# Attention, SwiGLU and maxout layers in one kernel: the first chunk's steps in another order, two more joint score runs, and some weight and softmax work moved between engines

## The chip, the cores and the metric

The kernel runs on one core of one Trainium2 chip. The metric is device time in microseconds. A program on a core drives five engines, each with its own queue of instructions that it works through in order: PE (matrix products), PEld (the same engine's weight loads, which run beside its products), DVE (VectorE), ACT (ScalarE), POOL (GpSimd) and SP (SyncE, which here only issues the transfers). Engines wait for each other and for transfers through semaphores.

## The reference

```python
attn = softmax(where(mask, q @ k.T / 8, -1e9)) @ v     # 4 batches, 8 heads, 576 rows, 64 wide
# heads 0..3: a window of the last 32 rows; heads 4..7: every 32nd row before this one
x = attn.transpose(0, 2, 1, 3).reshape(2304, 512)
g = x @ w_gate; x = (g * sigmoid(g) * (x @ w_val)) @ w_out       # 512 -> 1536 -> 512
out = max(x @ w1, x @ w2, x @ w3) @ w_out2                       # 512 -> 768 -> 512
```

All data is float32. The kernel makes each float32 product from three reduced-precision ones: an operand is split into a high part and a low part, and high times high, high times low and low times high are summed.

## The kernel before, in words

The 2304 rows of `x` are cut into five chunks of 512, 384, 512, 512 and 384 rows. The first chunk is special. No weight is in its final form yet, so while the first chunk is worked on, every weight tile of the SwiGLU layer is loaded as raw words, rounded, and split into its two parts; the later chunks then use them. At the same time the attention of the first two chunks goes through PE.

The order of this whole first stretch is written out by hand as a string, `FIRST`, of about 600 steps; `perform` runs each step once, and the instructions that a step issues are appended to the queues of their engines. So a step's place in the string is its place in every queue that it touches. A step is a letter and a number:

- Attention block i (15 of them; 0 to 3 strided and 4 to 7 local for chunk 0, 8 to 10 local and 11 to 14 strided for chunk 1): `l`/`m` load it (SP), `S` scores on PE (line 475), `M` masked maximum on DVE (line 498), `E` exponentials on ACT (506), `R` inverse of the sums on DVE (511, 512), `N` normalise on DVE or POOL (516), `T` transpose on PE (528), `V` copy out of PSUM on DVE or ACT (533, 535), `P` values product on PE (560), `H` high part of `x` on ACT or DVE (572, 574), `L` low part of `x` on DVE (578).
- Weight tile n (36 of them, in the order in which PE wants them; gate, value and output tiles are called g0, v0, g1, v1, o0, g2, v2, o1, and so on): `r` load the raw words (SP), `a` size (ACT, 291), `q` rounding (ACT, 294), `s` sign (ACT, 300, or POOL, 302), `c` clamp (POOL or DVE, 308), `t` shift (DVE, 314 or 316), `d` rounded sum (DVE, 320), `h` high part (ACT, 335), `o` low part (DVE or POOL, 340), `y` store to DRAM.
- The layer itself for tile f: `G`/`b` gate product on PE (748 to 750, into `ps_g`), `u` tanh on ACT (805), `w` silu on DVE (809), `B` value product on PE (`ps_v`), `x` their product on DVE (813), `z`/`j` high and low part (ACT 782, DVE 786), `O` output product on PE (`ps_y`).

A product of one tile is 12 matmuls of 512 columns: four steps of lines 748, 749 and 750, which need, in this order, the high parts of both operands, the low part of `x` (or of `h`), and the low part of the weight tile. `G0` is cut in two: `G0` does its first half, `b0` the second half after attention blocks 4 to 7 are done, and right behind it come `B0`, `G1`, `B1` and `O0`. Two PSUM buffers hold gate and value products, so `G1` can start when `w0` has read the product of `G0`.

`W` i scores blocks i and i + 1 in one run, with their products interleaved (`scores_beside`); the kernel before does so for blocks 13 and 14 alone.

Which engine does a step is set by seven tuples: `ON_SCALAR` (signs), `EVICT_ON_VECTOR` (`V`), `HIGH_ON_VECTOR` (`H`), `NORM_ON_POOL` (`N`), `CLAMP_ON_VECTOR` (`c`) and `LOW_ON_POOL` (`o`) among them. The string `LATER`, for the other chunks, and the last layer are the same in both kernels.

Of the kernel before, what the change touches and what calls it, by code (L numbers as in the profile page):

```python
# [51 lines left out]


FIRST = """
l0 k0 l1 l2 l3 l4 m4 k1 l5 m5 r0 l6 m6 l7 m7 r1 r2 r3 r4 S0 M0 S1 E0 M1 S2 R0 E1 N0 M2 S3 E2 R1 T0 M3 N1 S4 V0
E3 R2 T1 P0 N2 M4 V1 T2 R3 P1 E4 V2 N3 H0 S5 L0 T3 H1 M5 P2 V3 E5 L1 P3 R4 N4 H3 a0 S6 R5 q0 c0 L3 T4 H2 M6 N5
s0 t0 T5 L2 E6 S7 d0 V5 h0 M7 P5 V4 R6 E7 P4 o0 N6 G0 a1 R7 H5 N7 T6 H4 L5 a2 l8 L4 c1 T7 V6 q1 s1 r5 V7 q2 P6
c2 a3 P7 t1 H6 r6 q3 s2 L6 S8 H7 d1 s3 L7 c3 m8 h1 b0 t2 r7 a4 o1 q4 d2 a5 B0 t3 c4 r8 h2 M8 c5 u0 o2 s4 r9 w0
E8 d3 G1 x0 r10 h3 t4 t5 z0 o3 q5 y1 d4 a6 j0 s5 B1 R8 s6 l9 h4 d5 u1 r13 o4 q7 h5 N8 q6 w1 c6 O0 r12 a7 o5 s7
t6 x1 c7 m9 a8 d6 q8 r11 T8 t7 c8 z1 G2 V8 d7 h6 y3 j1 h7 o6 a9 o7 q9 r14 P8 s8 a10 c9 S9 u2 t8 l10 H8 B2 s9 M9  # L60
c10 y4 L8 a11 d8 E9 w2 c11 r15 t10 O1 x2 h8 q11 R9 m10 o8 z2 N9 r17 q10 t9 s11 T9 j2 G3 s10 d9 r16 t11 V9 d10 h9
d11 y7 a12 o9 h10 P9 h11 s12 B3 y6 u3 o10 H9 o11 q12 L9 c12 S10 a13 w3 y9 q13 c13 a14 t12 M10 s13 x3 c14 O2 r21
q14 s14 z3 t13 E10 d12 r18 d13 G4 j3 h12 R10 h13 r19 o12 a15 N10 q15 t14 y10 a16 T10 o13 u4 B4 d14 V10 w4 c15
r20 s15 c16 t15 q16 s16 h14 y12 d15 P10 a17 o14 q17 O3 x4 c17 H10 l11 h15 t16 r23 s17 L10 z4 d16 y13 o15 G5 h16
j4 q18 m11 l12 m12 o16 a18 r24 s18 t17 c18 a19 d17 S11 u5 y15 t18 c19 B5 w5 h17 M11 q19 r22 o17 a20 d18 E11 t19
s20 y16 x5 G6 c20 h18 R11 t20 z5 N11 s19 r26 j5 q20 T11 o18 a21 O4 d20 r25 V11 d19 q21 h20 c21 h19 o20 r27 s21
t21 P11 S12 o19 a22 B6 d21 H11 l13 l14 u6 c22 L11 y19 h21 s22 w6 q22 o21 q23 r28 t22 O5 a24 x6 s23 c24 m13 m14
d22 z6 y18 q24 s24 h22 j6 a23 o22 G7 r29 a25 M12 c23 q25 t24 E12 r31 t23 c25 d24 W13 s25 d23 y21 B7 h24 R12 M13
h23 N12 u7 y22 o23 E13 w7 t25 T12 M14 r32 a26 o24 O6 V12 R13 s26 x7 q26 c26 r30 a27 N13 z7 t26 q27 d25 P12 r33
a28 j7 G8 h25 d26 H12 o25 s27 L12 c27 y24 h26 c28 t27 a29 T13 o26 q29 r34 B8 d27 V13 s28 u8 s29 c29 w8 y25 t28  # L70
h27 q28 t29 o27 a30 O7 r35 x8 s30 q30 d28 z8 y27 c30 h28 j8 a31 o28 q31 G9 d29 q32 y28 s31 c31 t30 h29 t31 E14
d30 O8 d31 u9 o29 h30 R14 h31 o30 a32 N14 y30 a33 w9 B9 s32 q33 o31 a34 c32 y31 q34 c33 s33 t32 T14 a35 x9 c34
G10 V14 t33 s34 z9 d32 q35 j9 h32 d33 s35 P13 P14 o32 u10 B10 t34 h33 w10 c35 H13 H14 d34 L13 L14 h34 o33 O9 o34
y33 x10 t35 z10 y34 j10
"""
# [1255 lines left out]
```

## Time and profile before

| what | value |
|---|---|
| median of three runs | 779.96 us (779.40 to 781.55) |
| the profiled execution's own time | 779.35 us |
| its span, first to last instruction | 777.6 us, so 1.75 us lie around it |
| PE busy in the span | 763.9 us (98%) |
| DVE, ACT, POOL busy | 614.0, 457.3, 169.3 us |

The span is cut by what PE does: up to 23.74 us there is attention alone and PE often waits; from 23.74 to 34.92 us lies the first gate and value product; from 34.92 to 139.57 us the rest of the first chunk; behind it the other chunks and the last layer. A row of a timeline gives start, length, engine, line, operation, output and inputs, their shape, and in brackets the idle time ahead of it with what ended it. A matmul's length overlaps the next one's: what a matmul costs PE is the distance from its start to the next start.

### The profile page before, as it was taken

What the parts mean: (1) busy time and instruction counts of PE and PEld (TensorE: products, weight loads), DVE (VectorE), ACT (ScalarE), POOL (GpSimd) and SP (SyncE); (2) the same over time, 40 slices, a digit from 0 to 9 for tenths busy, and PEclk for the clock granted to TensorE, in tenths of its full rate; (3) what the DMA queues carried; (4) which work ended last, traced back from release to release, by engine and by line L of the source; (5) the groups of instructions that cost most, each with busy time, mean ns of one, the idle gap of its engine ahead of it and who ended that gap; (6) DMA issues with size and microseconds to landing.
All of it is one profiled execution on the core that took longest, in us unless ns stands there. A gap on an engine that the chain in (4) does not pass through costs nothing.

```text
span 777.6 us, 13127 instructions
## 1 busy us (share of the span) xinstructions
PE 763.9 (98%) x4644; PEld 695.2 (89%) x4644; DVE 614.0 (79%) x1218; ACT 457.3 (59%) x990; POOL 169.3 (22%) x165
## 2 busy tenths in 40 slices
PE   6999999999999999999999999999999999999998
PEld 4677788999988888888888999999999999999998
DVE  5999999888899989999999963626688377856683
ACT  6999997666857757477787752423345233443332
POOL 2434332111221121111121211411124011321120
PEclk9999999999999999999999999999999999999999
DMA  9979875576645976636978699996775976879722
GB/s 284 364 257 330 306 298 208 153 263 233 227 138 169 347 228 213 205 130 223 360 240 314 205 366 332 400 376 249 279 260 203 418 272 250 284 286 352 274 96 82
DMA packets 72290, 203.60 MB, mean 262 GB/s; under 512 B 8640, under 2 KB 40320, under 8 KB 67616
## 3 DMA queue, kind: packets, MB, share of 16 engines
q1 hardware_dynamic: 72224, 202.76, 73.7%
q8 instruction: 37, 0.61, 0.3%
q14 instruction: 29, 0.24, 0.1%
HBM read 158.69 MB, written 44.04 MB: 261 GB/s over the span
## 4 chain that ended last, share of the span: by engine, by line
PE 91%; DMA 3%; DVE 2%; ACT 2%; POOL 1%; issue 0%; SPq 0%; ACTq 0%; DVEq 0%
PE ps_a L913 19%; PE ps_c L913 10%; PE ps_v L748 6%; PE ps_y L748 6%; PE ps_g L748 6%; PE ps_y L749 6%; PE ps_y L750 6%; PE ps_g L750 6%; PE ps_v L750 6%; PE ps_g L749 6%; PE ps_v L749 6%; PE ps_b L913 5%; PE ps_a L560 1%; PE ps_a L528 1%; PE ps_a L475 1%; DMA qke<-in_locqk_dram 1%
## 5 line engine op out<-in xcount | busy, mean ns | idle before, releaser
L924 ACT ACTIVATE s<-ps_a 128x384 f32<-128x384 f32 x99 | 48.5, 490 | 132.9 <-PE ps_a L913 132.9
L786 POOL TENSOR_TENSOR hl<-ht,hh 128x512 fp32r<-128x512 f32 (+1 forms) x47 | 62.8, 1336 | 289.7 <-ACT hh L782 283.6
L748 PE MATMUL ps_g<-xh,wh_g 128*128 128x512 f32 (+1 forms) x240 | 90.2, 376 | 1.1 <-DVE ht L809 1.1
L748 PE MATMUL ps_v<-xh,w_v 128*128 128x512 f32 (+1 forms) x240 | 90.3, 376 | 0.5 <-DMA w_v<-wvdr 0.5
L748 PE MATMUL ps_y<-hh,w_o 128*128 128x512 f32 (+1 forms) x240 | 89.6, 373 | 0.0
L749 PE MATMUL ps_g<-xl,wh_g 128*128 128x512 f32 (+1 forms) x240 | 88.4, 368 | 0.2 <-DVE xl L578 0.2
L750 PE MATMUL ps_v<-xh,w_v 128*128 128x512 f32 (+1 forms) x240 | 88.4, 369 | 0.0
L750 PE MATMUL ps_y<-hh,w_o 128*128 128x512 f32 (+1 forms) x240 | 88.4, 368 | 0.0
L749 PE MATMUL ps_y<-hl,w_o 128*128 128x512 f32 (+1 forms) x240 | 88.4, 368 | 0.0
L750 PE MATMUL ps_g<-xh,wl_g 128*128 128x512 f32 (+1 forms) x240 | 88.4, 368 | 0.0
L749 PE MATMUL ps_v<-xl,w_v 128*128 128x512 f32 (+1 forms) x240 | 88.3, 368 | 0.0
L782 ACT ACTIVATE hh<-ht 128x512 fp32r<-128x512 f32 (+1 forms) x60 | 35.1, 585 | 41.2 <-DVE ht L777 30.2
L777 DVE SCALAR_TENSOR_TENSOR ht<-ht,ps_v 128x384 f32<-128x384 f32 (+1 forms) x48 | 29.6, 618 | 31.8 <-PE ps_v L750 28.5
L913 PE MATMUL ps_a<-y0hT,wr 128*128 128x384 f32 x162 | 54.1, 334 | 0.0
L913 PE MATMUL ps_a<-y1hT,wr 128*128 128x384 f32 x162 | 54.1, 334 | 0.0
L748 PEld LDWEIGHTS ps_g<-xh,wh_g 128*128 128x128 f32 x240 | 45.1, 188 | 7.5 <-DVE ht L809 1.5
L769 ACT ACTIVATE ht<-ps_g 128x384 f32<-128x384 f32 (+1 forms) x48 | 26.1, 545 | 43.1 <-PE ps_g L750 42.6
L748 PEld LDWEIGHTS ps_v<-xh,w_v 128*128 128x128 f32 x240 | 45.1, 188 | 6.9 <-issue 0.8
L750 PEld LDWEIGHTS ps_v<-xh,w_v 128*128 128x128 f32 x240 | 45.0, 188 | 6.2 <-DVE w_v L340 0.5
L750 PEld LDWEIGHTS ps_y<-hh,w_o 128*128 128x128 f32 x240 | 45.0, 188 | 6.0 <-DVE w_o L340 0.3
L749 PEld LDWEIGHTS ps_g<-xl,wh_g 128*128 128x128 f32 x240 | 45.1, 188 | 5.8 <-DVE xl L578 0.5
L750 PEld LDWEIGHTS ps_g<-xh,wl_g 128*128 128x128 f32 x240 | 45.1, 188 | 5.8
(255 smaller groups left out, 2062.4 us busy)
## 6 DMA issues: line engine op xcount, KB each, us to landing
wr<-wsdr SPq DMA_DIRECT2D x36, 1792.0 KB, 7.6
raw<-in_w_dram SPq DMA_DIRECT2D x60, 512.0 KB, 6.5
w_v<-wvdr SPq DMA_DIRECT2D x36, 512.0 KB, 5.7
w_o<-wodr SPq DMA_DIRECT2D x36, 512.0 KB, 4.4
wsdr<-whi SPq DMA_DIRECT2D x36, 256.0 KB, 4.2
wvdr<-w_v SPq DMA_DIRECT2D x12, 512.0 KB, 4.8
wodr<-w_o SPq DMA_DIRECT2D x12, 512.0 KB, 4.5
wsdr<-w SPq DMA_DIRECT2D x24, 256.0 KB, 3.7
```

Source lines behind the costliest of these rows:

```text
L475: yield nc.tensor.matmul(self.s[self.half[j], g], self.q[r, u, a], self.k[r, u, a], start=True, stop=True)
L528: nc.tensor.transpose(ps[:sm.shape[2], g * 128:(g + 1) * 128], sm[:, g], ident)
L560: ins = nc.tensor.matmul(ps[j * D:(j + 1) * D, at:at + nq], v, p, start=True, stop=True).ins
L748: nc.tensor.matmul(ps, wh, xh, start=first, stop=False)
L749: nc.tensor.matmul(ps, wh, xl, start=False, stop=False)
L750: nc.tensor.matmul(ps, wl, xh, start=False, stop=last)
L769: nc.scalar.activation(t, gates.pop((c, f)), AF.Silu)
L777: nc.vector.scalar_tensor_tensor(t, t, 1.0, vals.pop((c, f)), ALU.mult, ALU.mult)
L782: nc.scalar.activation(hs[c, f][0], t, AF.Copy)
L786: eng.tensor_tensor(hl, held.pop(("t", c, f)), f32(hh), ALU.subtract)
L913: nc.tensor.matmul(ps, w[:, c, a, ks], b, start=first and n == q == 0, stop=last and n == len(wts) - 1 and q == 2, skip_group_check=True,)
L924: nc.scalar.activation(s, ps, AF.Copy)
```

## The change

The string `FIRST` is replaced by another one with the same work in a new order, in which `W8` stands for `S8` and `S9`, and `W11` for `S11` and `S12`. The tuples change as follows.

```diff
-E3 R2 T1 P0 N2 M4 V1 T2 R3 P1 E4 V2 N3 H0 S5 L0 T3 H1 M5 P2 V3 E5 L1 P3 R4 N4 H3 a0 S6 R5 q0 c0 L3 T4 H2 M6 N5
-s0 t0 T5 L2 E6 S7 d0 V5 h0 M7 P5 V4 R6 E7 P4 o0 N6 G0 a1 R7 H5 N7 T6 H4 L5 a2 l8 L4 c1 T7 V6 q1 s1 r5 V7 q2 P6
-c2 a3 P7 t1 H6 r6 q3 s2 L6 S8 H7 d1 s3 L7 c3 m8 h1 b0 t2 r7 a4 o1 q4 d2 a5 B0 t3 c4 r8 h2 M8 c5 u0 o2 s4 r9 w0
+T1 P0 N2 T2 V1 M4 R3 E4 S5 P1 H0 V2 N3 a0 T3 M5 V3 P3 P2 L0 S6 R4 H1 c0 S7 L1 H3 E5 R5 m6 q0 N4 H2 s0 N5 m7 M6
+L3 t0 E6 T5 d0 T4 V5 M7 V4 R6 P5 L2 h0 P4 a1 N6 E7 R7 H5 L5 o0 G0 a2 T6 r6 H4 a3 V6 q4 N7 c1 T7 L4 q2 P6 q1 l8
+H6 s1 c2 V7 P7 q3 t1 L6 H7 c3 l9 d1 s3 s2 W8 t2 a4 r5 L7 d2 h1 m9 b0 o1 a6 t3 M8 B0 r9 a5 h2 u0 r11 w0 s4 o2 G1
...
-ON_SCALAR = (0, 3, 4, 5, 7, 9, 10, 11, 13, 15, 17, 18, 19, 21, 23, 25, 27, 29, 31, 33, 35)
+ON_SCALAR = (0, 3, 4, 5, 7, 9, 10, 11, 13, 15, 17, 18, 19, 21, 23, 25, 27, 29, 31, 32, 33, 34, 35)
...
-EVICT_ON_VECTOR = (0, 2, 3, 5, 6, 7)
-HIGH_ON_VECTOR = (0, 3)
-NORM_ON_POOL = (0, 1, 2, 3, 4, 5, 6, 7)
+EVICT_ON_VECTOR = (3, 5, 6, 7, 9, 14)
+HIGH_ON_VECTOR = (0, 3, 4, 11, 13)
+NORM_ON_POOL = (1, 3, 4, 5, 7, 8, 10, 12, 13)
...
-CLAMP_ON_VECTOR = ()
-LOW_ON_POOL = ()
+CLAMP_ON_VECTOR = (11, 23, 25, 27, 30, 34)
+LOW_ON_POOL = (0, 1, 3, 4, 6, 8, 16, 17, 19, 21, 29, 30, 32)
```

By these tuples the low parts of 13 weight tiles go from DVE to POOL, the clamps of 6 from POOL to DVE, and two signs from POOL to ACT; three normalisations go from POOL to DVE and four the other way.

First place: PE around `b0`, the second half of the first gate product. Before, the run of scores ahead of it is `S8` alone:

```order
L528 MATMUL ps_a<-cst,qke 96x128 x8
L560 MATMUL ps_a<-qke,ve 64x64 x16
L475 MATMUL ps_a<-loct 64x96 x8
L748 MATMUL ps_g<-xh,wh_g_433 128x512
L749 MATMUL ps_g<-xl,wh_g_433 128x512
```

Now it is `W8`:

```order
L528 MATMUL ps_a<-cst,qke 96x128 x8
L560 MATMUL ps_a<-qke,ve 64x64 x16
L475 MATMUL ps_a<-loct 64x96 x16
L748 MATMUL ps_g<-xh,wh_g_449 128x512
L749 MATMUL ps_g<-xl,wh_g_449 128x512
```

The 8 score products of block 9 have moved up into the run ahead of `b0`; their own run, after the second gate product of the dense stretch, is gone. In the same way the runs of blocks 11 and 12 become one run of 16 where block 11's was, and the run of block 10 now stands right behind `P9`, where it was one product later by itself.

Second place: POOL from the normalisation of block 7 (`qke`, 128x384, the last of its kind) on. `w32_...` is a weight tile in work: before, 475, 489, 518, 563 and 569 are v0, g1, v1, o0 and g2.

```order
L516 TENSOR_TENSOR qke_181<-qke_181,state_183 128x384
L308 TENSOR_SCALAR w32_475<-w32_475 128x512
L302 TENSOR_SCALAR raw_186<-raw_186 128x512
L308 TENSOR_SCALAR w32_489<-w32_489 128x512
L302 TENSOR_SCALAR raw_188<-raw_188 128x512
L308 TENSOR_SCALAR w32_518<-w32_518 128x512
L308 TENSOR_SCALAR w32_563<-w32_563 128x512
L308 TENSOR_SCALAR w32_569<-w32_569 128x512
```

Now 462, 482, 493, 497 and 603 are the same five tiles, and the row before the normalisation is the low part of g0:

```order
L340 TENSOR_TENSOR wl_g0_450<-w32_335,wh_g0_449 128x512
L516 TENSOR_TENSOR qke_192<-qke_192,state_194 128x384
L308 TENSOR_SCALAR w32_462<-w32_462 128x512
L302 TENSOR_SCALAR raw_204<-raw_204 128x512
L308 TENSOR_SCALAR w32_482<-w32_482 128x512
L308 TENSOR_SCALAR w32_493<-w32_493 128x512
L302 TENSOR_SCALAR raw_206<-raw_206 128x512
L340 TENSOR_TENSOR w_v0_567<-w32_462,w_v0_567 128x512
L308 TENSOR_SCALAR w32_497<-w32_497 128x512
L308 TENSOR_SCALAR w32_603<-w32_603 128x512
L308 TENSOR_SCALAR w32_578<-w32_578 128x512
L340 TENSOR_TENSOR w_v1_644<-w32_493,w_v1_644 128x512
```

The sign of g1 (`raw_206`, step `s2`) now has one more clamp ahead of it, that of v1, and the low parts of g0, v0 and v1 stand in this queue.

Third place: DVE at the same time. `xl` is the low part of `x`; before, the two `xl` rows are `L6` and `L7`, and `ps_a_520` is block 7's:

```order
L316 SCALAR_TENSOR_TENSOR w32_475<-w32_475,raw_186 128x512
L578 TENSOR_TENSOR xl_297<-ps_a_507,xh_296 128x2x128
L320 ISA w32_475<-w32_475,q_474 128x1024
L578 TENSOR_TENSOR xl_297<-ps_a_520,xh_296 128x2x128
L316 SCALAR_TENSOR_TENSOR w32_489<-w32_489,raw_188 128x512
L340 TENSOR_TENSOR w_v0_551<-w32_475,w_v0_551 128x512
L320 ISA w32_489<-w32_489,q_488 128x1024
L314 TENSOR_SCALAR w32_518<-w32_518 128x512
...
L340 TENSOR_TENSOR wl_g1_589<-w32_489,wh_g1_588 128x512
L809 SCALAR_TENSOR_TENSOR ht_598<-ht_598,ps_g_467 128x512
```

Now `ps_a_524` is block 7's:

```order
L316 SCALAR_TENSOR_TENSOR w32_462<-w32_462,raw_204 128x512
L578 TENSOR_TENSOR xl_295<-ps_a_508,xh_294 128x2x128
L320 ISA w32_462<-w32_462,q_461 128x1024
L316 SCALAR_TENSOR_TENSOR w32_482<-w32_482,raw_206 128x512
L578 TENSOR_TENSOR xl_295<-ps_a_524,xh_294 128x2x128
L320 ISA w32_482<-w32_482,q_481 128x1024
L314 TENSOR_SCALAR w32_493<-w32_493 128x512
...
L809 SCALAR_TENSOR_TENSOR ht_608<-ht_608,ps_g_474 128x512
L340 TENSOR_TENSOR wl_g1_606<-w32_482,wh_g1_605 128x512
```

`L7` has gone behind the shift of g1 (line 316 on `w32_482`), the low part of v0 has left this queue, and the silu of tile 0 (line 809) now stands ahead of the low part of g1.

## Rows read from the trace of the kernel before

**Rows 1.** The page's first part: busy time (share of the span) of each engine.

```profile
PE 763.9 (98%) x4644; PEld 695.2 (89%) x4644; DVE 614.0 (79%) x1218; ACT 457.3 (59%) x990; POOL 169.3 (22%) x165
```

**Rows 2.** Busy time by stage: PE, PEld, DVE, ACT, POOL, clock, DMA share, GB/s.

```profile
0.00:23.74 23.74, 15.94 (x240) 12.59 (x241) 14.44 (x97) 16.89 (x74) 5.52 (x15) 0.93 0.95 308
23.74:34.92 11.18, 9.68 (x84) 6.91 (x80) 10.25 (x26) 10.45 (x25) 8.00 (x9) 1.00 0.98 341
34.92:70.00 35.08, 34.77 (x206) 27.61 (x207) 34.02 (x73) 33.49 (x74) 13.19 (x16) 1.00 0.85 292
70.00:139.57 69.57, 69.49 (x460) 55.51 (x459) 67.20 (x140) 58.14 (x127) 22.58 (x28) 1.00 0.78 280
139.57:777.60 638.03, 633.97 (x3664) 592.61 (x3660) 488.13 (x885) 338.34 (x693) 120.03 (x99) 1.00 0.72 255
```

**Rows 3.** What PE waited for: us in total, times, longest.

```profile
PE ps_a L528 <- POOL qke L516: 1.6, 2, 1.0
PE ps_g L748 <- DVE ht L809: 1.1, 1, 1.1
PE ps_a L528 <- DVE sm L516: 0.3, 1, 0.3
```

**Rows 4.** PE's timeline: score runs of one block and of two.

```profile
47.27 0.88 PE L475 MATMUL ps_a<-loct 64*64 64x96 f32 x16
48.08 0.50 PE L748 MATMUL ps_v<-xh,w_v 128*128 128x512 f32 x1
48.41 0.39 PE L749 MATMUL ps_v<-xl,w_v 128*128 128x512 f32 x1
48.65 0.39 PE L750 MATMUL ps_v<-xh,w_v 128*128 128x512 f32 x1
...
76.98 0.67 PE L475 MATMUL ps_a<-loct 64*64 64x48 f32 x16
...
96.12 0.68 PE L475 MATMUL ps_a<-loct 64*64 64x48 f32 x32
...
138.75 0.89 PE L475 MATMUL ps_a<-loct 64*64 64x96 f32 x32
```

**Rows 5.** PE's timeline: second step of `b0`, and the start of `G1`.

```profile
29.33 0.50 PE L749 MATMUL ps_g<-xl,wh_g 128*128 128x512 f32 x1 [0.19 <-DVE xl L578]
34.92 0.50 PE L748 MATMUL ps_g<-xh,wh_g 128*128 128x512 f32 x1 [1.11 <-DVE ht L809]
```

**Rows 6.** DVE's timeline between `L7` and `w0`.

```profile
28.86 0.41 DVE L578 TENSOR_TENSOR xl<-ps_a,xh 128x256 fp32r<-128x256 f32 x1
29.49 0.69 DVE L316 SCALAR_TENSOR_TENSOR w<-w,raw 128x512 int32<-128x512 int32 x1 [0.21 <-POOL raw L302]
30.10 1.10 DVE L340 TENSOR_TENSOR w_v<-w,w_v 128x512 fp32r<-128x512 f32 x1
...
33.59 0.68 DVE L340 TENSOR_TENSOR wl_g<-w,wh_g 128x512 fp32r<-128x512 f32 x1
34.20 0.67 DVE L809 SCALAR_TENSOR_TENSOR ht<-ht,ps_g 128x512 f32<-128x512 f32 x1
```

**Rows 7.** POOL's timeline: the sign of g1, then three clamps in a row.

```profile
28.48 0.98 POOL L302 TENSOR_SCALAR raw<-raw 128x512 f32<-128x512 f32 x1
29.53 3.15 POOL L308 TENSOR_SCALAR w<-w 128x512 f32<-128x512 f32 x3
```

**Rows 8.** Two-operand work on POOL in later chunks: by form (busy, mean ns), and two single rows.

```profile
L786 POOL TENSOR_TENSOR hl<-ht,hh 128x512 fp32r<-128x512 f32 x24 | 36.2, 1506 | 164.0 <-ACT hh L782 164.0
...
238.85 1.29 POOL L786 TENSOR_TENSOR hl<-ht,hh 128x512 fp32r<-128x512 f32 x1 [5.99 <-ACT hh L782]
...
273.09 2.42 POOL L786 TENSOR_TENSOR hl<-ht,hh 128x512 fp32r<-128x512 f32 x1 [7.70 <-ACT hh L782]
```

**Rows 9.** DVE's timeline beside those two: one 128x1088 product each.

```profile
239.15 2.14 DVE L657 TENSOR_TENSOR pr<-stk,stq 128x1088 f32<-128x1088 f32 x1
...
273.06 1.28 DVE L688 TENSOR_TENSOR pr<-stv,stsc 128x1088 f32<-128x1088 f32 x1
```

More of the change, by code (lines that the diff above doesn't have):

```diff
@@ L54 @@
 FIRST = """
-l0 k0 l1 l2 l3 l4 m4 k1 l5 m5 r0 l6 m6 l7 m7 r1 r2 r3 r4 S0 M0 S1 E0 M1 S2 R0 E1 N0 M2 S3 E2 R1 T0 M3 N1 S4 V0
-E3 R2 T1 P0 N2 M4 V1 T2 R3 P1 E4 V2 N3 H0 S5 L0 T3 H1 M5 P2 V3 E5 L1 P3 R4 N4 H3 a0 S6 R5 q0 c0 L3 T4 H2 M6 N5
-s0 t0 T5 L2 E6 S7 d0 V5 h0 M7 P5 V4 R6 E7 P4 o0 N6 G0 a1 R7 H5 N7 T6 H4 L5 a2 l8 L4 c1 T7 V6 q1 s1 r5 V7 q2 P6
-c2 a3 P7 t1 H6 r6 q3 s2 L6 S8 H7 d1 s3 L7 c3 m8 h1 b0 t2 r7 a4 o1 q4 d2 a5 B0 t3 c4 r8 h2 M8 c5 u0 o2 s4 r9 w0
-E8 d3 G1 x0 r10 h3 t4 t5 z0 o3 q5 y1 d4 a6 j0 s5 B1 R8 s6 l9 h4 d5 u1 r13 o4 q7 h5 N8 q6 w1 c6 O0 r12 a7 o5 s7
@@ L60 @@
[L60 to L74, printed above, removed]
+l0 k0 l1 l2 l3 S0 l4 S1 k1 l5 r0 l7 l6 M0 r1 r2 E0 m5 M1 S2 E1 m4 R0 r3 S3 M2 r4 N0 E2 R1 T0 M3 R2 V0 S4 N1 E3
@@ new lines @@
+T1 P0 N2 T2 V1 M4 R3 E4 S5 P1 H0 V2 N3 a0 T3 M5 V3 P3 P2 L0 S6 R4 H1 c0 S7 L1 H3 E5 R5 m6 q0 N4 H2 s0 N5 m7 M6
+L3 t0 E6 T5 d0 T4 V5 M7 V4 R6 P5 L2 h0 P4 a1 N6 E7 R7 H5 L5 o0 G0 a2 T6 r6 H4 a3 V6 q4 N7 c1 T7 L4 q2 P6 q1 l8
+H6 s1 c2 V7 P7 q3 t1 L6 H7 c3 l9 d1 s3 s2 W8 t2 a4 r5 L7 d2 h1 m9 b0 o1 a6 t3 M8 B0 r9 a5 h2 u0 r11 w0 s4 o2 G1
+c4 d3 t4 E8 x0 r15 c5 c6 r7 r8 h3 d4 q5 o3 z0 s5 u1 h4 m8 s6 q8 t5 a7 r13 o4 B1 r10 c7 R8 d5 N8 j0 h5 q7 q6 O0
+t6 w1 o5 T8 x1 a8 d6 r12 s7 z1 c8 h6 q9 t7 d7 a10 M9 y3 V8 s8 j1 G2 h7 t8 a9 r14 o6 y4 a11 o7 P8 B2 u2 s9 l10 w2
@@ new lines @@
+d8 H8 c10 r17 c9 c11 L8 O1 x2 E9 y1 h8 o8 t10 q11 R9 z2 N9 q10 T9 y6 G3 t9 s10 s11 d9 t11 h9 V9 a12 P9 d11 d10
+m10 o9 q17 s12 h11 j2 S10 y7 h10 u3 H9 o11 L9 c12 q12 B3 o10 a13 O2 r20 q13 w3 c13 a14 y9 t12 M10 c14 x3 G4 s13
+r16 E10 r19 t13 q14 z3 d12 r18 r21 s14 d13 h12 R10 q15 j3 o12 N10 h13 T10 t14 a16 o13 a15 c15 u4 B4 w4 l11 q16
+c16 y10 y13 d14 s15 V10 h14 y12 t15 d15 a17 o14 P10 O3 x4 a21 s16 t16 s17 H10 r23 l12 h15 c17 G5 z4 d16 h16 q18
+m11 o16 a18 a19 s18 c18 t17 u5 L10 j4 o15 d17 l13 W11 y15 c19 r28 t18 r24 B5 h17 m12 M11 o17 t19 w5 q19 r22 a20
@@ new lines @@
+d18 G6 E11 s20 x5 q20 c20 R11 z5 t20 r26 N11 h18 r30 d20 T11 j5 s19 O4 r25 q21 d19 h20 r27 h19 y16 V11 c21 s21
+t21 o20 o19 o18 a22 d21 P11 s22 H11 L11 u6 h21 w6 l14 B6 q22 q23 c22 t22 a24 s23 x6 q24 o21 z6 a23 y19 y18 O5
+d22 c24 j6 h22 s24 t24 m13 r29 m14 o22 a25 G7 M12 c23 c25 q25 E12 t23 d24 s25 u7 W13 r31 d23 t25 R12 h23 M13 B7
+N12 y21 o23 y22 E13 w7 T12 M14 r32 h24 a26 V12 O6 q26 R13 a31 P12 o24 x7 c26 a27 s26 N13 z7 d25 h25 q27 a28 t26
+d26 r33 c27 G8 s27 q29 H12 h26 c28 o25 a29 t27 u8 d27 L12 T13 V13 o26 s28 c29 j7 B8 y24 s29 w8 q30 t29 t28 q28
@@ L75 @@
+h27 a30 O7 x8 s30 d28 d29 z8 c31 r35 h28 a32 c30 q31 j8 o28 G9 t30 r34 o27 E14 O8 s31 h29 u9 q33 y28 d30 t31 y27
+h30 R14 a33 d31 h31 N14 w9 q32 B9 x9 o29 o31 s32 q34 c32 s33 c33 a34 T14 o30 t32 q35 G10 z9 a35 V14 t33 d32 c34
+j9 s34 P14 P13 H13 d33 h32 c35 s35 t34 H14 u10 B10 d34 w10 t35 o32 L14 y30 O9 h34 h33 o33 x10 o34 z10 y25 L13
+y34 j10 y31 y33
 """
```

## The prediction, on record before the result

> **What bounds the kernel now.** I read the busy times first: PE is busy for 763.9 us [rows 1]. The table by stage says where the rest is [rows 2]. Behind 139.57 us PE idles for 4.1 of 638 us; the steps there are the same in both kernels, so what the first chunk gains or loses there is simply added to the end. From 34.92 to 139.57 us PE idles for 0.31 + 0.08 us. The idle time that this change can reach lies before: 7.8 us up to 23.74, and 1.5 us (11.18 - 9.68) between 23.74 and 34.92. Most of the 7.8 us is the wait for the first transfers and then a chain of small softmax steps.
>
> So there are two questions. Does PE get less to do in the first chunk? And do the engines that make the weights still deliver in time? The second is tight: from 34.92 to 70 us DVE is busy for 34.02 of 35.08 us and ACT for 33.49 [rows 2]. They are as full as PE, and only PE's own order hides it. From 70 us on ACT falls to 84% (58.14 of 69.57) and POOL has room throughout.
>
> The waits name two narrow places [rows 3]: `G1` waited 1.1 us for the silu of tile 0, and a transpose 0.3 us for the normalisation of block 9 on DVE. The DVE rows show why the silu was late [rows 6]: the shift of g1 waited until the sign of g1 on POOL ended (28.48 + 0.98 = 29.46 [rows 7]); then the low part of v0 took 1.02 us from start to next start instead of 0.6, because three clamps ran on POOL beside it; the low part of g1 and the silu followed, and the silu ended at 34.8. `G1` started at 34.92 [rows 5].
>
> **The change part by part.** *Joint runs.* A run of one local block lasts 0.88 us and one of two 0.89; one of a strided block 0.67 and one of two 0.68 [rows 4]. A run overlaps the next matmul by 0.07 (47.27 + 0.88 against 48.08). `W8` and `W11` each save one run: 0.81 + 0.60 = **-1.4 us** of PE time. The bounds are these rows; nothing else in PE's work changes, since the other runs only stand elsewhere.
>
> *Interruptions.* Behind a score run the first matmul costs 0.33 us to the next start, the second 0.24 [rows 4]: an interruption costs 0.1 us. Block 10's scores now stand behind another small run, so the stretch has one interruption less, as the new order on PE shows: **-0.1 us**. Blocks 9 and 12 stood beside other small runs already.
>
> *Block 9.* Its scores come some 18 us earlier (47.27 [rows 4] against the 29.33 of [rows 5], ahead of which `W8` stands), its maximum and exponentials some steps earlier on DVE and ACT. The 0.3 us that its transpose waited go: **-0.3 us**, bounds -0.3 and 0. `W8` takes both PSUM buffers of this kind; the one of block 9 is given back by its maximum, ahead of `V8` on DVE, and only `P8` is queued for it, so I put that at nothing. If the maximum is late, `P8` and all PE work behind it wait.
>
> *The start, 23.74 to 34.92.* This is the term that I can bound and not fix. In the new order `L7` stands behind the shift of g1 on DVE, and that shift needs the sign of g1 on POOL. Let X be the time at which that sign ends. Then come the shift (0.6, start to start), `L7` (0.34, from the 0.41 of its row less the overlap), the five remaining steps of `b0` (5 x 0.23) and `B0` (12 x 0.23): G1 starts at X + 4.9. DVE no longer holds it up, since the low part of v0 (1.02) has left its queue and the silu stands 0.6 us further ahead. Before, X was 29.46 and `G1` came at 34.92, so the new order breaks even at X = 30.0.
>
> What is X now? Ahead of that sign POOL has one clamp more (between 0.6 and 1.05; the three clamps in 3.15 us are the upper end [rows 7]) and the low part of g0 (1.29 to 2.42, mean 1.51 [rows 8]), but no longer the normalisation of block 6, and the scores of blocks 6 and 7 stand together on PE, ahead of the transposes of 4 and 5. I followed the new rows of all engines with these durations twice, once with the scores at the start slow and every POOL row beside DVE at its upper end, once without: X = 30.1 and X = 28.8. I take the middle, 29.5: **-0.5 us**. The bounds: 1.5 us better if all idle time of this stage goes, and 2 us worse if X is 32 (below).
>
> *Lows on POOL, clamps on DVE.* Thirteen lows leave DVE, 0.6 us each. But beside a two-operand POOL instruction a 128x1088 product on DVE took 2.14 us; beside another it took 1.28, and then the POOL instruction took 2.42 instead of 1.29 [rows 8, 9]. Whichever loses, one of them loses about a microsecond. At 0.86 us lost on DVE for each 0.6 us taken off it, 13 lows make DVE's work 3.4 us longer; at none lost, 7.8 us shorter. The lows of DVE stand between instructions that read PSUM, so I take half the loss: DVE gains 13 x (0.6 - 0.43) = 2.2 us in 100. The six clamps cost it 0.34 us each, a shift's length (2.0 us), and spare it the same collisions. So DVE comes out level. This is where a rule of the Trainium skill speaks against the change: GPSIMD Engine Reference, "Key points", says that GpSimd shares its SBUF interfaces with VectorE and contends with its instructions that have two SBUF inputs. The trace agrees, with the 2.14 against 1.28 us; by the rule alone DVE would take the whole loss, which is the slower rival below.
>
> *The rest of ACT, DVE, POOL.* ACT gets two evictions and two signs, and gives up two evictions and three high parts; POOL gives up three normalisations and gets four. Level again, so ACT stays at 95% until 70 us, and can run ahead by no more than its idle 1.6 us. PE, 2 us earlier, will meet a tile that is not ready: I charge **+0.4 us**, bounds 0 and 1.3 (all that is gained before 70 us: 0.81 + 0.1 + 0.3, rounded up).
>
> *Transfers.* The raw words of v0 and g1 go ahead of the values of blocks 4 to 7. By the shapes, 5.07 MB are queued up to the values of block 4, at 308 GB/s [rows 2] some 16.5 us, and they are needed at about 21; those of 6 and 7 are 6.51 MB, 21.1 us, needed at 26. The raw words of o1 and g3 go behind those of three later tiles, 1.5 MB or 5 us, and are not wanted before 41 us. Nothing, if that holds.
>
> Sum: -1.4 - 0.1 - 0.3 - 0.5 + 0.4 = **-1.9 us**. The profiled execution took 779.35 us (777.6 and 1.75 around it), so 777.45; the median of the runs is 0.6 above it: **778.0 us**, 0.25% less. A measurement of this kernel tells no less than about 0.3% (2.3 us) from no change.
>
> **The rivals.** *The start gains too* (chance 0.36). X is 28.5 or less, all idle time between 23.74 and 34.92 goes (-1.5), and the weights keep up: -1.4 - 0.1 - 0.3 - 1.5 = -3.3, 776.7 us. For it: DVE has 1.6 us less ahead of the silu. Against: three full engines before 70 us.
>
> *The weights set the pace* (0.16). PE waits for ACT and DVE until 70 us and only `W11` and the lost interruption remain: -0.7, 779.3 us. For it: the 97% and 95% [rows 2]. Against: PE hardly waited before, at the same load.
>
> *GpSimd holds the start* (0.11, slower). Every POOL row beside DVE takes its upper end, the low of g0 2.42 us and each clamp and sign 1.05. From 25.3 us for the first clamp, 1.1 later for that low, five rows of 1.13: X = 32.05, `G1` at 36.95, +2.0. Then three more clamps, the lows of v0, v1 and o0 at 2.5 and a sign follow X: 12 us, 44.1, where `O0` wants the last at 42.9: +1.2 more. With -1.8 from the first three terms: +1.4, 781.4 us, and 782.4 where two further lows (v2, g3) lose 0.5 us each. It decides from X = 31.8 on, where the start has lost all of the -1.8. For it: the two rows of rows 8. Against: the low of g0 leaves POOL before the softmax of block 7 is there.
>
> **How the numbers follow.** My forecast has 0.37, and its own range is 777.0 to 779.0. Faster by over 0.3% is the first rival and the edge of the forecast: 0.38. Slower is the last one, which reaches 782.3 only in part; with what I have not seen, 0.11. Within 0.3%: 0.51. The range leaves out 0.1 at either end: 776.2 to 780.8.
>
> **What would show it.** In the changed profile: score runs of 0.89 and 0.68 us at `W8` and `W11`; no wait of the transpose for block 9; the end of the sign of g1, and `G1` 4.9 us behind it; `L749` of `b0` waiting for `L7`; lows on POOL of 1.3 to 2.4 us. I am wrong if PE waits for a low part on POOL (line 340) for more than half a microsecond in all, if PE idles for over 1 us between 35 and 70 us, or if anything behind 139 us changes its length.

## The result: slower, and the profile after

The changed kernel takes 784.91 us (median of six runs, 783.75 to 787.11) where the kernel before takes 779.83: a ratio of 1.0056, 95% interval 1.0035 to 1.0078. The forecast was 778.0, and its range ended at 780.8. The profiled execution is the longest of the six: 787.11 us, span 785.3.

The page's first part gives busy time (share of the span) of each engine; PE does its 763 us of work as in [rows 1], and the span is 7.7 us longer.

```profile
PE 763.2 (97%) x4644; PEld 694.3 (88%) x4644; DVE 618.3 (79%) x1213; ACT 458.0 (58%) x989; POOL 186.5 (24%) x171
```

Cut at the same times as [rows 2], with the same columns:

```profile
0.00:23.74 23.74, 15.16 (x245) 12.11 (x246) 15.38 (x101) 18.80 (x81) 5.36 (x14) 1.00 0.95 320
23.74:34.92 11.18, 9.01 (x96) 6.94 (x95) 9.37 (x24) 9.48 (x24) 8.88 (x10) 1.00 1.04 364
34.92:70.00 35.08, 32.77 (x186) 26.07 (x185) 34.77 (x68) 32.61 (x69) 23.23 (x20) 1.00 0.77 268
70.00:139.57 69.57, 67.39 (x420) 52.85 (x420) 67.58 (x137) 58.56 (x125) 29.84 (x30) 1.00 0.71 264
139.57:785.30 645.73, 638.83 (x3703) 596.38 (x3701) 491.19 (x888) 338.51 (x693) 119.19 (x99) 1.00 0.72 254
```

From 34.92 to 139.57 us PE idles for 2.31 + 2.18 us where it idled for 0.39. DVE has given 13 low parts away and is busier than before: 34.77 of 35.08 us against 34.02. That row is the prediction's failure in one line. What PE waits for from `G1` on (us, times, longest), where [rows 3] had 0.3 us:

```profile
PE ps_a L528 <- DVE sm L516: 1.8, 2, 1.1
PE ps_y L749 <- DVE hl L786: 0.9, 2, 0.8
PE ps_g L748 <- ACT sm L506: 0.9, 1, 0.9
PE ps_a L560 <- ACT w_o L335: 0.9, 1, 0.9
```

By place, with the waits as PE's timeline brackets them: `O0` 0.76, `P8` 0.85, `T9` 0.69, `G6` 0.87, `T14` 1.11, `O10` 0.17. Two of these are put down to ACT, at `P8` and `G6`; both went when nothing but DVE steps was put forward ("Three places of the order" below). No wait names a low part on POOL (line 340): the harm goes through DVE. In POOL's timeline (start, length) the sign of g1 ends at 29.15, and four low parts follow, those beside `b0`, `O0`, `T9` and `T14`:

```profile
28.49 0.66 POOL L302 TENSOR_SCALAR raw<-raw 128x512 f32<-128x512 f32 x1
29.36 1.65 POOL L340 TENSOR_TENSOR w_v<-w,w_v 128x512 fp32r<-128x512 f32 x1 [0.22 <-ACT w_v L335]
...
38.38 1.85 POOL L340 TENSOR_TENSOR w_o<-w,w_o 128x512 fp32r<-128x512 f32 x1 [0.45 <-ACT w_o L335]
...
41.34 1.15 POOL L516 TENSOR_TENSOR sm<-sm,stat 128x384 f32<-128x384 f32 x1
...
52.20 1.57 POOL L340 TENSOR_TENSOR wl_g<-w,wh_g 128x512 fp32r<-128x512 f32 x1 [2.93 <-ACT wh_g L335]
...
57.04 3.10 POOL L302 TENSOR_SCALAR raw<-raw 128x512 f32<-128x512 f32 x1 [3.26 <-ACT w L291]
...
120.99 1.60 POOL L340 TENSOR_TENSOR w_v<-w,w_v 128x512 fp32r<-128x512 f32 x1
```

And DVE's timeline at the same moments:

```profile
38.99 1.79 DVE L786 TENSOR_TENSOR hl<-ht,hh 128x512 fp32r<-128x512 f32 x1
...
41.72 0.68 DVE L809 SCALAR_TENSOR_TENSOR ht<-ht,ps_g 128x512 f32<-128x512 f32 x1
...
52.54 1.26 DVE L511 TENSOR_SCALAR stat<-stat 128x4 f32<-128x4 f32 x1
...
57.73 0.68 DVE L340 TENSOR_TENSOR w_v<-w,w_v 128x512 fp32r<-128x512 f32 x1
58.33 0.68 DVE L786 TENSOR_TENSOR hl<-ht,hh 128x512 fp32r<-128x512 f32 x1
58.93 0.68 DVE L340 TENSOR_TENSOR wl_g<-w,wh_g 128x512 fp32r<-128x512 f32 x1
...
121.37 1.43 DVE L516 TENSOR_TENSOR sm<-sm,stat 128x192 f32<-128x192 f32 x1
```

Read them in pairs by their ends. The low part of 38.38 ends at 40.23; the `hl` of 38.99, which alone takes 0.68, ends at 40.78, and `O0` goes on at 40.84. The one of 52.20 ends at 53.77; a sum over four columns, 0.16 us alone, ends at 53.80, and `T9` is late by what follows. The one of 120.99 ends at 122.59; the normalisation of block 14 at 122.80. A DVE instruction that starts while POOL works ends a fixed time after POOL's, 0.55 us for two 512-column inputs, 0.28 for one, 0.02 for four columns: it waits until POOL has ended, and then does its own work. All 38 DVE rows between 24 and 142.60 us that are over 0.05 us longer than the shortest of their form end in this way. The silu at 41.72, one of whose inputs lies in PSUM, takes its 0.68 us beside POOL's 41.34. And at 57.04 it is POOL that waits, 3.10 us for a sign, while DVE works without a gap.

### The profile page after: what moved, and what is told of

It is laid out like the page before. It is cut to its first block, busy times and chain, and to the rows that moved or that the text cites. A ratio compares the mean times of both kernels' runs of the same rounds, so it can differ in the third digit from the quotient of the medians.

```text
span 785.3 us, 13096 instructions
## 1 busy us (share of the span) xinstructions
PE 763.2 (97%) x4644; PEld 694.3 (88%) x4644; DVE 618.3 (79%) x1213; ACT 458.0 (58%) x989; POOL 186.5 (24%) x171
## 4 chain that ended last, share of the span: by engine, by line
PE 80%; DVE 2%; DMA 1%; ACT 1%; issue 0%; SPq 0%; ACTq 0%; DVEq 0%
PE ps_a L913 19%; PE ps_c L913 10%; PE ps_y L749 5%; PE ps_y L748 5%; PE ps_v L748 5%; PE ps_y L750 5%; PE ps_v L750 5%; PE ps_v L749 5%; PE ps_g L748 5%; PE ps_b L913 5%; PE ps_g L750 5%; PE ps_g L749 5%; DMA wsdr<-s 1%; PE ps_a L560 1%; PE ps_a L528 1%; PE ps_a L700 1%
## 5 line engine op out<-in xcount | busy, mean ns | idle before, releaser
L320 DVE CUSTOM_DVE_ANT_0 w<-w,q 128x1024 uint16<-128x1024 uint16 x60 | 50.9, 854 | 4.2 <-ACT q L300 2.5
L748 PEld LDWEIGHTS ps_v<-xh,w_v 128*128 128x128 f32 x240 | 45.2, 188 | 9.6 <-DVE y0lT L268 2.9
L749 PEld LDWEIGHTS ps_y<-hl,w_o 128*128 128x128 f32 x240 | 45.4, 189 | 7.5 <-DVE hl L786 2.2
```

Source lines behind the costliest of these rows:

```text
L320: nc.vector.tensor_tensor(w, w, q, ALU.add)
L748: nc.tensor.matmul(ps, wh, xh, start=first, stop=False)
L749: nc.tensor.matmul(ps, wh, xl, start=False, stop=False)
```

## Experiments

Behind each text: the median, the ratio to the kernel before on the same chip (95% interval), and **the stretch**, the time from the start of `G1` to the start of chunk 1. The stretch is the sharpest measure here: two executions of the kernel before's first chunk gave 104.65 and 104.62 us, two of the changed one's 108.36 and 108.44. The start of `G1` scatters far more (33.17 to 34.92 for the same first chunk), and so do the runs. The stretch has a limit too: it leaves out what is lost ahead of `G1`, and where `G1` came at 37 us or later, in three of the runs below, the makers of the weights had 2 to 4 us more for their work.

**Lows back on VectorE.**

```diff
-LOW_ON_POOL = (0, 1, 3, 4, 6, 8, 16, 17, 19, 21, 29, 30, 32)
+LOW_ON_POOL = ()
```

> The changed kernel with its 13 low parts of weight tiles back on VectorE. Theory A (the low parts on GpSimd slow the two-operand instructions of VectorE beside them, and PE waits for what is queued behind): the 4.1 us of new waits between 35 and 140 us go, chunk 1 starts near 138.5 us instead of 142.6, and the time is 777 to 780 us. Theory B (the new order puts single steps too late, whatever engine makes the low parts): the waits ahead of P8, T9, G6 and T14 stay, 783 to 786 us. Theory C (VectorE has too much to do in either case, 7.8 us more of it here): slower than the change, 786 to 790 us.

785.65 us, 1.0072 (1.0050 to 1.0094), stretch 108.13. Not A: the order wants them away from DVE. The waits ahead of `P8`, `T9` and `T14` are gone; `O0` waits 1.17 us, `G6` 0.52 and other places 1.44, which is 3.13 in all, and all but the 0.52 is named after DVE. So most of B's waits aren't there, although the time lies in its range, and C's range begins above it: none of the three fits, and C's reason, too much work on DVE, comes nearest. Ahead of the stretch PE waited 2.06 us at 25.83 for the low part of g0, now on DVE; the granted clock was then 0.55 from 24 to 28 us and 0.59 from 28 to 32, and `G1` came at 37.13.

**Order alone**: all tuples of the kernel before, the new `FIRST`.

> The new order and joint runs with all tuples of the kernel before (no low part and the clamps on GpSimd). Theory A: 777 to 779.5 us, since the joint runs save 1.4 us and nothing slows VectorE. Theory B: 783 us or more, with PE idle for over 2 us between 35 and 140 us.

783.72 us, 1.0049 (1.0032 to 1.0066), stretch 107.48. The order by itself costs 2.8 us of the stretch, with 1.62 us ahead of `O0`, 0.52 ahead of `G6`, 0.47 for a low part on DVE, and none ahead of `P8`, `T9` and `T14`:

```profile
43.18 0.50 PE L749 MATMUL ps_y<-hl,w_o 128*128 128x512 f32 x1 [1.62 <-DVE hl L786]
```

Ahead of the stretch PE waited 2.01 us for the low part of g0 here too; with that low part on POOL, in the changed kernel, it didn't wait for it.

**Tuples alone**: the `FIRST` of before, all new tuples.

> The order of the kernel before with all tuples of the changed one (13 low parts on GpSimd, 6 clamps on VectorE, and so on). Theory A: 783 to 787 us, PE idle for 3 us or more between 35 and 140 us, behind VectorE instructions of 1.4 to 1.9 us. Theory B: 779 to 781 us, as the kernel before.

783.68 us, 1.0045 (1.0029 to 1.0061), stretch 108.07. Both halves cost: here 2.01 us ahead of `T9`, 0.68 ahead of `T14`, nothing ahead of `G6`. A and B are each half of it, and the halves overlap (2.8 and 3.4 against 3.7 together).

**Joint runs alone**, from the kernel before; the load `l9` and `M9` move ahead too.

```diff
-q3 s2 L6 S8 H7
+q3 s2 l9 L6 W8 H7
...
-c19 a19 d17 S11 u5
+c19 a19 d17 W11 u5
```

> The kernel before with the two joint score runs alone (and the loads and the masked maximum of block 9 earlier, which they need). Theories A and B alike: 1.4 us of score runs less, and the 0.3 us ahead of the transpose of block 9, so 778.1 us; if an earlier run of block 9 holds a buffer or VectorE up, PE idles for the same 1 to 2 us elsewhere between 30 and 55 us, and the time is 779 to 781 us.

781.81 us, 1.0028 (1.0011 to 1.0046), stretch 104.20. A mishap of the edit: PE waited 2.49 us at 30.52 for the load of block 9, and 1.15 ahead of `T9`, whose exponentials had stayed where they were. The stretch is the shortest of all, but `G1` came at 37.22, so it doesn't show that the saved runs are kept.

**Three places of the order**, in the changed kernel.

```diff
-R8 d5 N8 j0 h5
+j0 R8 d5 N8 h5
...
-q9 t7 d7 a10 M9 y3
+q9 M9 t7 d7 a10 y3
...
-h17 m12 M11 o17 t19 w5 q19
+h17 m12 w5 M11 o17 t19 q19
```

> The changed kernel with three VectorE steps earlier in the order: the low part of the hidden tile 0 ahead of the inverse and the rounded sum that stood before it, the silu of tile 5 ahead of the masked maximum of block 11, and the masked maximum of block 9 ahead of two shifts' worth of weight steps. Theory O (these three places of the new order made the waits ahead of O0, P8 and G6): those waits, 0.76 + 0.85 + 0.87 us, go; chunk 1 starts near 140.1 us and the median is near 782.4 us. Theory V (VectorE is late as a whole, and any step put forward makes the next one late): the waits turn up at other places, chunk 1 starts at 142 us or later, 784 to 786 us.

785.71 us, 1.0074 (1.0053 to 1.0094), stretch 107.32. The waits ahead of `O0`, `P8` and `G6` are gone, 2.48 us, and the stretch is 1.04 shorter: `T9` now waits 1.58 (from 0.69) and `T11` 0.59. The median is no better than that of the changed kernel. That is V more than O: with DVE full, a step put forward makes another late.

**Low parts in quarters.** Each low part on GpSimd in four instructions.

```diff
-        lo_eng.tensor_tensor(lo, w32, f32(hi), ALU.subtract)
+        step = 128 if lo_eng is nc.gpsimd else 512
+        for c in range(0, 512, step):
+            lo_eng.tensor_tensor(lo[:, c:c + step], w32[:, c:c + step], f32(hi)[:, c:c + step], ALU.subtract)
```

> The changed kernel with each of its 13 low parts on GpSimd done in four instructions of 128 columns instead of one of 512. Theory L (a VectorE instruction that starts beside one of GpSimd waits until that one has ended): it now waits for a quarter at most, so what the VectorE rows beside low parts are longer than alone falls from 12.6 us to under 6 us, the waits ahead of T9 and T14 shrink, chunk 1 starts 1 to 2.5 us earlier than 142.6, 782 to 784 us. Theory B (the two engines share a bandwidth, byte for byte): the 12.6 us stay, the time stays at 784 to 786 us. If four short instructions are much longer in all than a long one, PE waits for a low part on GpSimd and the time rises.

782.58 us, 1.0038 (1.0025 to 1.0051), stretch 107.30. POOL's and DVE's timelines at one low part (line numbers are two higher here):

```profile
44.78 3.07 POOL L342 TENSOR_TENSOR w_v<-w,w_v 128x128 fp32r<-128x128 f32 x4
```

```profile
44.93 0.86 DVE L788 TENSOR_TENSOR hl<-ht,hh 128x512 fp32r<-128x512 f32 x1
45.72 0.95 DVE L316 SCALAR_TENSOR_TENSOR w<-w,raw 128x512 int32<-128x512 int32 x1
46.59 0.94 DVE L342 TENSOR_TENSOR w_o<-w,w_o 128x512 fp32r<-128x512 f32 x1
```

The same bytes, and DVE loses 0.2 to 0.3 us at a time where it lost 1.1: the two take turns. Added over all DVE rows beside low parts (each less the shortest of its form), the loss falls from 12.6 us to 5.5; the waits ahead of `T9` and `T14` are gone. That is L, and not B. The quarters have a price on POOL: the low parts take 35.0 us there instead of 19.8, and PE now waits for POOL, 1.32 us ahead of `T8` and 0.21 for a low part:

```profile
43.06 0.42 PE L530 MATMUL ps_a<-cst,sm 128*96 128x128 f32 x2 [1.32 <-POOL sm L518]
```

**Lows on GpSimd alone**, in the kernel before.

```diff
-LOW_ON_POOL = ()
+LOW_ON_POOL = (0, 1, 3, 4, 6, 8, 16, 17, 19, 21, 29, 30, 32)
```

> The kernel before with the 13 low parts on GpSimd and nothing else changed. Theory L: each low part holds VectorE up by about 1 us and takes 0.6 us off it, so PE waits for VectorE (ahead of T9 and T14 above all, 2 to 4 us in all between 35 and 140 us), 782 to 784 us. If it was the other tuples (clamps, high parts, normalisations) that made these waits in the run with all tuples: 779 to 780.5 us.

782.36 us, 1.0028 (1.0011 to 1.0045), stretch 106.97, 2.3 more than before, with 1.63 us ahead of `T9` and 0.54 ahead of `T14`. The low parts make two thirds of what all tuples cost. Ahead of the stretch PE waited 1.14 us for the low part of v0 on POOL, in the place of the 1.11 for the silu: in the old order a low part on POOL does hold PE itself.

**Joint runs, mended.** As above, with `l9` behind `l8`, and `E9`, `R9` and `N9` some steps earlier.

> The kernel before with the two joint runs alone, now with the loads of block 9 right behind those of block 8, and its exponentials, inverse and normalisation ahead of some weight steps. By the terms of the prediction: 1.4 us of score runs and the 0.3 us wait less, nothing else, chunk 1 starts near 137.9 us, 778.2 us. If the block's earlier steps make weight steps late on ScalarE or VectorE: new waits of 1 to 2 us between 45 and 60 us, 779.5 to 781 us.

780.22 us, 0.9999 (0.9985 to 1.0013), stretch 104.68. In the stretch the score runs take 2.86 us instead of 4.23, so 1.37 are saved as foreseen; PE gives it all back: 0.43 us for a low part of DVE ahead of `G3`'s third matmul, 0.15 and 0.20 at two more places, and the rest in gaps too short to be bracketed (the matmuls of the products take 0.85 us more from start to start).

**An earlier reload, in the kernel before.** In the last chunk PE waited 0.53 us at 492.93 for a value tile. Only the load's place is changed (`LAST`).

```diff
-yl0 ou4.6 mu4.7 hi4.7 lo4.7 ga4.8 va4.8 si4.8 rv4.9 ro4.9 rv4.10
+rv4.9 yl0 ou4.6 mu4.7 hi4.7 lo4.7 ga4.8 va4.8 si4.8 ro4.9 rv4.10
```

> The kernel before with one transfer moved: the load of value tile 9 for the last chunk, for which PE waited 0.53 us at 492.93 us, is issued ahead of the loads of y and not behind them. Theory R (that load comes by luck early or late in a full DMA queue, and in most executions PE waits 0.5 to 2.7 us for it): the wait goes, 778 to 779.5 us, and the runs lie closer together than the 7 us that they spanned. If the loads of y are now late instead, or if the spread is made elsewhere: 780 us, and as wide.

777.90 us, 0.9983 (0.9972 to 0.9993), stretch 104.62. PE waits for nothing behind the first chunk, and twelve runs span 3.2 us (776.75 to 779.91) where 24 of the kernel before span 6.6. In equal numbers: the five sets of twelve with this move span 2.8 to 3.4 us, the four without it 3.2 to 7.3.

**The same in the changed kernel.**

> The changed kernel with the same one transfer moved. Theory R: the 2.62 us wait of its last chunk and the slower clock behind it go, behind the first chunk both kernels take the same time, and it stands 3.0 us (2.5 to 3.5) above the kernel before with the same move, 781.5 to 783 us. If something else behind the first chunk is longer in the changed kernel: 784 us or more, 5 us above that kernel.

782.67 us, 1.0036 (1.0015 to 1.0057), stretch 108.44, no wait behind the first chunk either. From the start of chunk 1 to PE's last matmul it takes 633.70 us, the kernel before with the same move 633.68. So the whole difference of the two kernels is made ahead of chunk 1, and R holds in that, though not in its 3.0 us. The medians stand 4.8 apart (4.1 by the ratios): the profile of before, from which I had taken 3.0, had a late `G1` (34.92; with the same first chunk, 33.17 here).

**Mended joint runs, clamps and signs on GpSimd in halves** of 256 columns. The clamp's edit is shown; the sign's is alike.

```diff
-        eng.tensor_scalar(w, w, W_MAX * scale, W_MIN * scale, ALU.min, ALU.max)
+        for h in (w[:, :256], w[:, 256:]) if eng is nc.gpsimd else (w,):
+            eng.tensor_scalar(h, h, W_MAX * scale, W_MIN * scale, ALU.min, ALU.max)
```

> The kernel before with the mended joint runs, and each clamp and sign on GpSimd in two instructions of 256 columns. With the joint runs alone PE had 1.4 us less to do between 35 and 140 us and took as long as before. Theory W (VectorE sets the pace there, and it loses some 12 us waiting for clamps and signs to end): the loss falls to 6 to 9 us, the gain of the joint runs stays, chunk 1 starts near 137.8 us and the time is 778.5 us. Theory S (ScalarE sets the pace): chunk 1 starts near 139.2 us as without the halves, 780 us.

779.48 us, 1.0007 (0.9990 to 1.0025), stretch 104.32. DVE's loss beside POOL fell from 11.6 to 8.1 us, the stretch by 0.36. Up to 70 us DVE waits 1.1 us for the high part of `x` on ACT, as it did without the halves, and ACT 1.2 for DVE instead of 1.9. That is nearer to S, whose 139.2 us for chunk 1 fits the 139.29: of 3.5 us that DVE no longer loses, PE gets a tenth.

**All mends in the changed kernel**: quarters, halves, three moves.

> The changed kernel with the low parts on GpSimd in quarters, its clamps and signs in halves, and the three VectorE steps earlier. Theory W: the waits of VectorE for GpSimd were most of the loss and the three places the rest; apart the two mends gave 2.2 and 0.3 us of chunk 1's start, and together 3 to 4 us: chunk 1 starts near 139 us, as in the kernel before, 780 to 781.5 us. If the new order is bounded by something else (ScalarE, or GpSimd itself, which is now the busier): chunk 1 starts at 140.4 us or later, 782.5 us.

786.14 us, 1.0092 (1.0064 to 1.0119), stretch 107.79: a miss of both theories, and most of the time is lost ahead of the stretch. The table by stage, its last three columns PE's granted clock, DMA share and GB/s:

```profile
28.00:32.00 4.00, 1.44 (x33) 1.03 (x33) 1.89 (x4) 3.05 (x6) 3.78 (x8) 0.87 1.03 348
32.00:36.00 4.00, 3.87 (x9) 3.09 (x10) 2.68 (x13) 1.96 (x4) 3.63 (x9) 0.50 1.03 371
36.00:40.00 4.00, 4.00 (x15) 3.15 (x15) 2.77 (x5) 2.91 (x12) 2.57 (x5) 0.77 0.75 236
```

PE waited 1.23 us for a load and 1.86 for `L7`, and then ran at half its clock (0.50 of 2.4 GHz): `B0` took 4.33 us instead of 2.72, and `G1` starts at 38.76. Inside the stretch the mends, worth 1.1 and 1.0 us apart, give 0.57 together: PE now waits 1.35 us at 85.40 for a low part on POOL, one of those in quarters, and 0.95 ahead of a score run. So theory W fails there too; which of the mends stands in the way is not shown.

**Earlier reload, `W11` alone, and the silu of tile 0 first.**

```diff
-c5 u0 o2 s4 r9 w0
+c5 u0 w0 o2 s4 r9
...
-c19 a19 d17 S11 u5
+c19 a19 d17 W11 u5
```

> The kernel before with the earlier load of value tile 9, the joint run of blocks 11 and 12 alone, and the silu of tile 0 ahead of the low part of gate tile 1 on VectorE. If a saved run is kept where VectorE and ScalarE have some room (from 70 us on ScalarE is at 84%): 0.6 us of scores less, and about 0.55 of the 1.1 us that the second gate product waits: 776.8 us, from gate product 1 to chunk 1 104.0 us. If the weights take it back there too: that stretch stays at 104.6 us, and the time is 777.4 us.

777.66 us, 0.9967 (0.9952 to 0.9982), stretch 104.80. The wait ahead of `G1` falls from 1.11 to 0.47, and inside the stretch the saved run is taken back, 0.29 us of it at the third matmul of `O0`.

**Earlier reload and both joint runs.**

> The kernel before with the earlier load and both joint runs, the mended ones. Theory P (weights and VectorE set the pace between 35 and 140 us, so that what the joint runs save comes back as small waits): the stretch from gate product 1 to chunk 1 stays at 104.7 us and the time is that of the earlier load alone, 777.5 to 778.2 us. If the joint runs are worth their 1.4 us, and the late wait hid it in the run without the earlier load: 776.5 us.

778.27 us, 0.9976 (0.9959 to 0.9994), stretch 104.57. P: nothing is kept of 1.4 us.

**Earlier reload and quarters, in the changed kernel.**

> The changed kernel with the earlier load and its low parts on GpSimd in quarters. Theory L (waits of VectorE for the end of a GpSimd instruction): 1.1 us less in the stretch from gate product 1 to chunk 1, as in the run without the earlier load, and 1 to 2.3 us less than the 782.67 us of the changed kernel with the earlier load: 780.4 to 781.7 us. If the quarters had gained by their luck in the last chunk alone: 782.5 us.

781.53 us, 1.0014 (0.9998 to 1.0030), stretch 107.30: 1.1 us less in both, as L says.

**Earlier reload and lows on GpSimd, in the kernel before.**

> The kernel before with the earlier load and the 13 low parts on GpSimd. Theory L: 2.3 us more from gate product 1 to chunk 1 and nothing else, 780.2 us against the 777.9 us of the earlier load alone. If the low parts cost nothing: 778 us; if they cost the whole of what the changed kernel lost: 781.5 us or more.

780.56 us, 1.0002 (0.9984 to 1.0020), stretch 106.91, 2.3 above the 104.62. PE's waits in the stretch (us, times, longest):

```profile
PE ps_a L528 <- DVE sm L516: 1.6, 1, 1.6
PE ps_a L528 <- ACT w L291: 0.5, 1, 0.5
```

By the medians 2.7 us, by the ratios (1.0002 and 0.9983) 1.5. So the low parts alone cost about 2 us.

## Why the prediction was wrong, step by step

**The failed step is "So DVE comes out level".** In the sum it stands at nothing; DVE was busy for 618.3 us instead of 614.0. I took half the loss for each low part, 0.43 us of 0.86. In the changed kernel 13 DVE rows beside low parts (the low part is what they overlap longest) are 12.6 us longer than alone, 0.97 for each, against 0.6 taken off. Clamps, signs and normalisations on POOL make another 9.4, where they made 12.5 before. My bound "13 lows make DVE's work 3.4 us longer" was near the truth (12.6 - 7.8 = 4.8), and I halved it because DVE's low parts stand between instructions that read PSUM. Those are indeed spared, but they are too few. I had read [rows 8, 9] as two engines slowing each other; the ends of the rows would have shown that one waits for the other's whole instruction: in the first pair DVE ends 1.15 us behind POOL (241.29 and 240.14), in the second POOL ends 1.17 behind DVE (275.51 and 274.34). The prediction also says that DVE's whole loss is its slower rival. It is not: that rival prices what POOL loses at the start, which didn't come, and a slower DVE is priced nowhere beyond the gains that it would take back.

The Trainium skill has this rule, on a page that the prediction didn't use: SBUF — State Buffer, "SBUF: two separate sides", says that the shared port pair is an exclusive lock and not a split of bandwidth, so that the engine that comes second is blocked for the other's whole instruction. The trace agrees, with the 0.55 us behind POOL's end; the quarters, which shorten the lock and not the bytes, agree too. By that rule a low part of 1.3 to 1.9 us would have been charged up to its whole length; of 19.8 us in all, 12.6 came to pass.

**The second is the pace, charged at 0.4 us with a bound of 1.3.** In the terms of the sum this is where the time went: 4.15 us of new waits were measured for it. The bound said that no more can be lost than is gained. That is wrong: it counted what PE gains, and not what the makers of the weights lose by a new order. The stretch grew by 3.71 us: 4.15 of new waits, 0.7 of gaps too short to be bracketed, 0.3 in transposes and value products, less 1.38 of score runs. Order alone gives +2.8, tuples alone +3.4, low parts alone +2.3. With DVE at 97% and ACT at 95% [rows 2], little idle time of PE meant that a hand-made order fitted, not that there was room. How the 3.7 us divide between order and tuples stays open, since the halves add up to 6.2; which steps of the new order cost its 2.8 was tried at three places only.

**Joint runs: the size was right, the worth was not.** 4.23 us of score runs became 2.85 in the stretch. Ahead of it `W8` took 1.20 us and not the foreseen 0.89, 0.3 more than `S8`; that cost nothing, since PE then waited for `L7`, which the prediction had named as a sign:

```profile
26.99 1.20 PE L475 MATMUL ps_a<-loct 64*64 64x96 f32 x32
28.12 0.50 PE L748 MATMUL ps_g<-xh,wh_g 128*128 128x512 f32 x1
30.26 0.50 PE L749 MATMUL ps_g<-xl,wh_g 128*128 128x512 f32 x1 [1.64 <-DVE xl L578]
```

But kept by itself in the kernel before, the gain comes to nothing (two executions: 104.68 and 104.57). "Does PE get less to do?" was the wrong question for a stretch in which PE waits as soon as it is earlier. The rival "the weights set the pace" named this, and priced it as the lost gain only.

**Block 9**: `T9` waits 0.69 us and not 0; `P8`, whose buffer I put at nothing, waited 0.85 until `M9` stood earlier.

**The start**: the sign of g1 ended at 29.15 (I took 29.5, and 32 for the slower rival), and `G1` came 5.1 us behind it (I said 4.9): the mechanism is right. The gain is not shown: 34.24 against 34.92 in the two profiles, but 34.77 against 33.17 in two others of the same first chunks. Executions differ there by more than the term.

**Behind 139 us**: "the steps there are the same" is true, and yet this execution took 4.27 us longer from chunk 1 to the last matmul. PE waited 0.35 and 2.62 us in the last chunk, against 0.53 before, and ran at a lower clock behind it. PE's timeline, and the stage around it:

```profile
498.67 0.41 PE L748 MATMUL ps_v<-xh,w_v 128*128 128x384 f32 x1 [2.62 <-DVE y0lT L268]
```

```profile
493.00:503.00 10.00, 7.38 (x35) 7.09 (x34) 4.34 (x8) 3.24 (x9) 3.73 (x3) 0.85 1.01 379
```

The named DVE row is not the cause: with `rv4.9` issued earlier the wait is gone in both kernels. The load stands in SP's queue while the DMA share is 1.01, and the wait came out between 0.5 and 2.8 us in the twelve profiles without that edit. It is no part of the change; it made this execution the longest. What remains of the 4.8 us (or 4.1) between the two kernels with the early load, beyond the 3.8 of the stretch, is not pinned down; the starts of `G1` scatter by more than that.

## What to carry to other kernels

Before an instruction is moved from VectorE to GpSimd, compare the ends of rows: if VectorE's rows end a fixed time behind GpSimd's, charge the move with up to GpSimd's whole duration (here two thirds of it), and weigh shorter GpSimd instructions against what they add on GpSimd (35.0 us for 19.8). Where three engines were at 95% or more, less work for one of them was worth nothing by itself here; look for the waits that lie outside that stretch, as the one transfer here that was worth 0.17% (777.90 us, faster than both kernels) and narrowed the scatter. And compare stretches between two fixed events, with an eye on when they start: they agreed to 0.1 us where whole runs scattered by 5.

## What the runs showed that I had not expected

A wait of PE can cost more than its length, through the clock: in the run with all mends `B0` took 1.6 us longer behind its waits. In the kernel before, PE waited 0.62 and 0.96 us at 18.16 and 19.76, and the granted clock was then 0.50 (1.2 GHz) from 20 to 22 us; the same first chunk with waits of 0.62 and 0.97 at 16.86 and 18.47 kept 1.00. After alike waits one execution fell and another didn't. It is a part of the scatter of `G1`: from the second wait's end on the first took 15.16 us to `G1` and the other 14.70. The slow row, of the kernel before:

```profile
20.00:22.00 2.00, 2.00 (x20) 1.48 (x18) 1.78 (x4) 1.48 (x6) 0.00 (x0) 0.50 1.02 416
```

The same window in the kernel before with the earlier reload:

```profile
20.00:22.00 2.00, 1.45 (x33) 1.39 (x34) 1.97 (x12) 2.00 (x8) 0.37 (x1) 1.00 1.02 413
```

And a VectorE instruction as small as 128x4 is held up like a large one: 1.26 us (the row of 52.54) instead of 0.16.
